# A token-group relabelling, a new vector order, and a reordered first and last pair in a convolution and SwiGLU kernel

## Chip, cores and metric

The kernel runs on one core of one Trainium2 chip. The metric is device microseconds of one execution. TensorE (PE) does the matmuls; VectorE (DVE), ScalarE (ACT) and GpSimd (POOL) work on 128-partition tiles; DMAs are issued from the queues of SyncE (SP), ScalarE and GpSimd. Everything is float32.

## The reference

```
w   = softmax(weight, axis=-1)                       # weight: 8 heads x 7 taps
y   = causal conv of x with w, one set of taps per head of 24 channels   # x: 8 x 4096 x 192
rms = sqrt(mean(y*y, axis=-1) + 1e-6)                # y as 32768 tokens x 192
xn  = y / rms * rms_g
g, val = xn @ w_gate, xn @ w_val                     # 192 x 1536 each
out = (g * sigmoid(g) * val) @ w_out                 # 1536 x 192
```

## The kernel before

**Pairs.** The 32768 tokens are cut into 32 pairs of 1024 tokens, each of two groups of 512. Pair 0 is computed plainly: `plain` (its matmuls are L1110) makes gate and value products, ScalarE the silu, VectorE the product of both, and `outer` (L1151) the output product; its results leave PSUM by a ScalarE copy (L1159) and a VectorE sum (L1163). Pairs 1 to 31 go by a bilinear scheme that needs fewer multiplications: sums of input columns ("X sums", XSUM, `x_sum` L718), of input weights (`w_sums` L375, negations L371) and of output weights (`out_sums` L914, negations L910) are formed, TensorE multiplies them, and sums of the products give the wanted values.

**One scheme pair on TensorE.** `Pair.products` yields 180 steps: 120 product steps (`Unit.product`, L823: four units u of hidden channels, 15 products i each, on two halves of the partitions), then 60 output steps (L1002), one for each word of OUTS. A word "n.u" multiplies form n of unit u by output weights; the forms (LEFT) are either the six gated blocks a to f of a unit or sums of them (SUMS: ab, cb, be, df, de, p4, p9, abe, abd, bce, bcf). The gated blocks are six (three columns of hidden channels for each of two token groups); PLACE says which block is which, and which token group is stored as g.

**The order of everything else.** ORDER is a string of words between the PE steps. "p3" is three PE steps. Another word has an engine letter and a name: V, P and W are VectorE, A ScalarE, G GpSimd, Q an accumulating DMA issued from GpSimd's queue (L1025; it reads one tile from SBUF and adds it to another), D a DMA of SyncE. A word that ends in "-" is for the pair before the current one (its tail: JOIN L1049, TURN transposes L1015, stores, and the convolution, norm, and X sums that feed later pairs). `AS`, `AF` copy PSUM (L772), `VC`, `VD`, `VN`, `VR` are VectorE sums (VR: L857), `AG` is silu (L869), `GM`/`VM` the gate product (L877), `Gab.0` and the like form sums (L1027). `Ak...` copies a summand to PSUM with ScalarE (`stage`, L726) so that the `P` sum on VectorE reads one operand there. `Asq`, `Vred`, `Gpow`, `Vbc`, `Gmul` and `Dplace` are the norm two pairs ahead (L498, L509 to L511, L515 to L521, L528, L536, L676), `cv` the convolution taps (ScalarE starts one, L474, VectorE adds six, L482), `GX1` and so on the X sums of the next pair, `load`, `fetA`, `fetB` DMAs. Each engine runs its own instructions in the order in which they were written, and waits where an input is not there. So the place of a word relative to others of its engine, and to the PE steps that use it, sets what waits.

**First pair and head.** START is a string of one-letter steps, one piece each: p, s, v are product, silu and value product of the plain pair, w four operations of `w_sums`, i, o, O weight conversions, c, n, t convolution, norm and placing of pair 1. LATER puts further steps at times of a list kept in `put`/`emit`, and so do the lines behind it for `part_tap`, `x_sum` and `out_sums` (12 of its 18 operations at `base + 2600 + 60 * i`; the rest inside pair 1's loop, one each ten PE steps after step 30). The list's numbers only order the work; they are not times on the chip.

**Last pair.** The loop runs one pass more than there are pairs, and the pass behind the last pair issues only the words that end in "-". In the last pair both stores, `st0` and `st1`, use ScalarE's queue for every second transfer.

Of the kernel before, what the change touches and what calls it, by code (L numbers as in the profile page):

```python
# [19 lines left out]
def kernel(  # L20
# [76 lines left out]
    ORDER = (
        "VD6- VD0- GX5- GX10- p1 VT2- p1 GX9- VD2- VD3- VT4- p2 VT5- Asq- AS40.0.0 p2 AS40.1.0",
        "VT3- p1 AF0.0.0 VT0- GX8- p1 VT1- VC.0.0 GX7- AF0.1.0 p3 VC.1.0 AS41.0.0 AS41.1.0 p1",
        "AS00.0.0 p2 AS00.1.0 p2 GX4- p1 Vred- VD5.1.0 AS42.0.0 VD5.0.0 p1 AS42.1.0 VR1.0.0",  # L100
        "VR0.0.0 Gpow- VR1.1.0 AS51.0.0 p1 AS51.1.0 p1 VR0.1.0 p1 Dload- Vbc- AF2.0.0 p1 AG0.0.0",
        "AF3.0.0 AG1.0.0 VN.1.0 p1 VR2.0.0 GM0.1.0 p1 AF3.1.0 p2 AG2.0.0 AS44.1.0 VR2.1.0 p2",
        "Dst1- p1 VS44.0.0 p1 VR3.0.0 p2 AS40.0.1 VR3.1.0 AS40.1.1 p1 GM1.1.0 VR5.0.0 Gmul-",
        "AG4.0.0 GM2.1.0 VR5.1.0 VM4.1.0 AG3.0.0 p1 AF0.0.1 p1 GM3.1.0 p2 Gcb.0 p1 VS41.0.1 p1",
        "AF0.1.1 VC.0.1 p1 AS41.1.1 VC.1.1 AS00.1.1 AG5.0.0 p1 VS00.0.1 p2 AS42.1.1 VS42.0.1",
        "VD5.0.1 AS51.0.1 p1 VD5.1.1 GM5.1.0 p1 AS51.1.1 p1 Gab.0 p2 VR1.0.1 p1 VR1.1.1 p1",
        "AF2.0.1 p1 AF2.1.1 VR0.0.1 p1 VR0.1.1 AG0.0.1 Qbe.0 VF3.0.1 Gdf.0 p3 VR2.0.1 GM0.1.1 p1",
        "AF3.1.1 VR2.1.1 p1 AG1.0.1 AS44.0.1 AS44.1.1 p1 VR5.0.1 AG5.0.1 GM1.1.1 p1 VR3.0.1 p1",
        "AS40.0.2 p2 VR5.1.1 VS40.1.2 p1 VR3.1.1 p2 Gde.0 p3 AG4.0.1 GM5.1.1 AF0.0.2 VM4.1.1",
        "VF0.1.2 AG3.0.1 VC.0.2 AS41.0.2 p2 VC.1.2 AS41.1.2 AG2.0.1 p1 AS00.0.2 p1 VS42.0.2 Gab.1",  # L110
        "p1 GM3.1.1 AS00.1.2 AS42.1.2 p2 VD5.0.2 p4 VD5.1.2 VR1.0.2 AS51.0.2 GM2.1.1 p1 VR1.1.2",
        "AS51.1.2 p2 VR0.0.2 AF2.0.2 p1 AF2.1.2 p1 VR0.1.2 p1 AG1.0.2 AG0.0.2 AF3.1.2 Gcb.1 p1",
        "VF3.0.2 VR2.0.2 VR2.1.2 AS44.0.2 p1 Gdf.1 Qde.1 GM1.1.2 VR5.0.2 AS44.1.2 VR5.1.2 p3",
        "AG2.0.2 p4 VR3.0.2 VS40.1.3 GM0.1.2 AS40.0.3 AG5.0.2 AG4.0.2 VR3.1.2 p1 AF0.0.3 p1",
        "AS41.0.3 p2 Gab.2 VM4.1.2 VF0.1.3 VC.0.3 p1 GM2.1.2 p1 VC.1.3 AS41.1.3 p4 GM5.1.2",
        "VS42.0.3 p1 AS00.0.3 AS00.1.3 VD5.0.3 VD5.1.3 p1 AG3.0.2 Gcb.2 AS42.1.3 p1 VR1.0.3",
        "VR1.1.3 p1 Dst0- AS51.0.3 AS51.1.3 p1 Gdf.2 Gp4.1 AF2.0.3 p1 AF2.1.3 AG1.0.3 VR0.0.3 p1",
        "VR0.1.3 p2 AF3.0.3 AF3.1.3 VS44.0.3 VR5.0.3 p1 GM3.1.2 p1 AG0.0.3 p1 AS44.1.3 VR2.0.3 p2",
# [1254 lines left out]
```

## Time and profile before

| | before |
|---|---|
| median of 3 runs | 2606.48 us (2603.78 to 2611.65) |
| the profiled execution's own time | 2604.78 us |
| its span in the profile | 2602.9 us |
| mean granted TensorE clock | 0.999 |
| busy: PE, DVE, POOL, ACT | 99%, 93%, 92%, 72% of the span |
| PE starts of scheme pairs 1, 2, 3, 4, 31 | 125.0, 212.3, 291.5, 371.4, 2516.5 us |
| last matmul starts, span ends | 2594.64 us, 2602.9 us |

In lines of the profile the columns are: start (in a timeline) or nothing, busy us, engine, line of the kernel, operation, output <- input by name, shape, and count; the square bracket is the engine's idle time before it and what ended that. In the list of waits: what waited, on which line, for which producer, us in total, number of waits, the longest.

### The profile page before, as it was taken

To read this page: it belongs to the slowest core of one execution; us is meant where nothing else is said; L and a number is where in the kernel's file an instruction comes from. 1 tells how busy PE (TensorE), PEld (TensorE's weight loads), DVE (VectorE), ACT (ScalarE), POOL (GpSimd) and SP (SyncE) were. 2 spreads that over 40 slices of the span, in tenths; PEclk is the share of its full clock that TensorE was granted. 3 is DMA by queue.
4 is the path that set the end of the run, shared out by engine and by line. 5 is a ranking of instruction groups with operands and counts; after the bars stand their busy time and mean duration, and the time that the engine had idled before them with its cause. 6 is when DMAs were issued, how large, how long until landed. Compare 5 with 4: busy or idle time off the path is not lost.

```text
span 2602.9 us, 61832 instructions
## 1 busy us (share of the span) xinstructions
PE 2564.1 (99%) x23128; PEld 1467.9 (56%) x23128; DVE 2424.1 (93%) x4056; ACT 1877.9 (72%) x3505; POOL 2398.9 (92%) x2104
## 2 busy tenths in 40 slices
PE   9999999999999999999999999999999999999998
PEld 6855555655555556555555555655556555645554
DVE  8889999999999999999999999999999999999976
ACT  6577777777777777677777777777778777787765
POOL 4899999999999999899999999999999999999987
PEclk9999999999999999999999999999999999999999
DMA  6243554444544445444455444455444455443432
GB/s 144 57 81 67 104 97 87 85 77 90 104 91 82 79 75 104 92 86 87 72 98 104 90 81 76 81 104 96 88 85 77 89 104 91 82 83 71 90 78 50
DMA packets 528490, 226.28 MB, mean 87 GB/s; under 512 B 456638, under 2 KB 459198, under 8 KB 528190
## 3 DMA queue, kind: packets, MB, share of 16 engines
q1 hardware_dynamic: 481004, 140.53, 27.4%
q0 software_dynamic: 44496, 81.02, 18.5%
q8 instruction: 182, 2.98, 0.5%
q10 hardware_dynamic: 2690, 0.79, 0.1%
q14 instruction: 118, 0.97, 0.1%
HBM read 83.84 MB, written 49.55 MB: 51 GB/s over the span
## 4 chain that ended last, share of the span: by engine, by line
PE 71%; POOL 15%; DMA 5%; issue 3%; DVE 2%; ACT 2%; SPq 0%; POOLq 0%; DVEq 0%; ACTq 0%
PE ps L823 51%; PE ps L1002 16%; POOL ht L877 5%; POOL nt L1027 3%; POOL early L1027 3%; PE ps L1110 2%; DMA early<-ht 2%; DMA more<-early 2%; PE ps L1151 1%; POOL tls L1027 1%; DMA xb<-xd 1%; POOL more L1025 1%; POOL more L1027 1%; ACT ps L772 0%; ACT ps L726 0%
## 5 line engine op out<-in xcount | busy, mean ns | idle before, releaser
L823 PE MATMUL ps<-xc,wf 64*128 64x512 f32 x4960 | 1398.1, 592 | 0.9 <-ACT tile L772 0.8
L823 PEld LDWEIGHTS ps<-xc,wf 64*128 64x128 f32 x4960 | 683.2, 187 | 462.4 <-issue 269.6
L823 PE MATMUL ps<-xb,wf 64*128 64x512 f32 x2480 | 864.9, 590 | 0.0
L772 ACT ACTIVATE tile<-ps 128x512 f32<-128x512 f32 (+1 forms) x749 | 416.3, 572 | 201.9 <-PE ps L1002 100.1
L823 PEld LDWEIGHTS ps<-xb,wf 64*128 64x128 f32 x2480 | 375.9, 187 | 241.0 <-issue 179.5
L772 ACT ACTIVATE ps<-ps 128x512 f32<-128x512 f32 (+1 forms) x713 | 383.1, 546 | 176.8 <-PE ps L1002 148.2
L772 ACT ACTIVATE tls<-ps 128x512 f32<-128x512 f32 (+1 forms) x615 | 344.1, 572 | 168.7 <-PE ps L1002 83.8
L877 POOL TENSOR_TENSOR ht<-ht,tile 128x512 f32<-128x512 f32 x312 | 438.8, 1471 | 22.0 <-ACT tile L869 21.1
L1002 PE MATMUL ps<-ht,x 128*32 128x256 f32 x5952 | 413.0, 380 | 0.0
L877 POOL TENSOR_TENSOR ht<-ht,tls 128x512 f32<-128x512 f32 x246 | 349.0, 1468 | 22.8 <-ACT tls L869 22.0
L1027 POOL TENSOR_TENSOR early<-early,ht 128x512 f32<-128x512 f32 x248 | 351.3, 1527 | 0.0
L482 DVE SCALAR_TENSOR_TENSOR ps<-xh,tp,ps 128x512 f32<-128x512 f32 x450 | 337.3, 751 | 15.1 <-ACT ps L474 8.8
L1027 POOL TENSOR_TENSOR early<-ht 128x512 f32<-128x512 f32 x248 | 342.7, 1382 | 4.8
L1002 PE MATMUL ps<-early,x 128*32 128x256 f32 x4216 | 278.9, 379 | 0.1
L1002 PEld LDWEIGHTS ps<-ht,x 128*32 128x32 f32 x5952 | 192.1, 110 | 130.1 <-DVE ht L877 4.9
L857 DVE TENSOR_TENSOR tile<-ps,tile 128x512 f32<-128x512 f32 x344 | 233.0, 684 | 11.0 <-ACT tile L772 6.3
L869 ACT ACTIVATE tile<-tile 128x512 f32<-128x512 f32 x344 | 213.9, 625 | 7.6 <-DVE tile L857 4.4
L857 DVE TENSOR_TENSOR ht<-ps,tile 128x512 f32<-128x512 f32 x310 | 209.9, 680 | 0.7 <-ACT tile L772 0.5
L857 DVE TENSOR_TENSOR tls<-ps,tls 128x512 f32<-128x512 f32 x276 | 187.3, 684 | 8.6 <-ACT tls L772 5.0
L726 ACT COPY ps<-ht 128x512 f32<-128x512 f32 x248 | 145.3, 589 | 60.2 <-DVE y L482 44.9
L1002 PEld LDWEIGHTS ps<-early,x 128*32 128x32 f32 x4216 | 136.6, 110 | 91.9 <-ACT ps L772 5.0
L869 ACT ACTIVATE tls<-tls 128x512 f32<-128x512 f32 x276 | 171.8, 625 | 6.0 <-DVE tls L857 3.6
(174 smaller groups left out, 3897.3 us busy)
## 6 DMA issues: line engine op xcount, KB each, us to landing
xb<-xd SPq DMA_DIRECT2D x120, 384.0 KB
ht<-ht POOLq DMA_DIRECT2D x93, 256.0 KB, 3.9
early<-ht POOLq DMA_DIRECT2D x93, 256.0 KB, 4.6
xd<-yn SPq DMA_DIRECT2D x244, 96.0 KB
out_dram<-o_sb SPq DMA_DIRECT2D x244, 96.0 KB
xh<-in_x_dram SPq DMA_DIRECT2D x192, 105.0 KB
more<-ht POOLq DMA_DIRECT2D x62, 256.0 KB, 3.3
more<-early POOLq DMA_DIRECT2D x31, 256.0 KB, 3.9
```

Of the source, the lines that this page charges most:

```text
L482: nc.vector.scalar_tensor_tensor(out=dst, in0=xk, scalar=w, in1=at, op0=ALU.mult, op1=ALU.add)
L726: nc.scalar.copy(out=bank(*at)[:], in_=src)
L772: nc.scalar.activation(out=dst, in_=src, func=AF.Copy, scale=float(s))
L823: nc.tensor.matmul(out=self.new(v, h, True) if first else self.old(v, h), lhsT=wf[self.u][HALF[h], WAT[i], :], rhs=x_op(XOP[i])[HALF[h]], ...
L857: nc.vector.tensor_tensor(out=dst, in0=self.old(v, h), in1=t[:], op=plus(s))
L869: nc.scalar.activation(out=t[:], in_=src[:], func=AF.Silu)
L877: engine[eng].tensor_tensor(out=self.hv(v), in0=src, in1=t[:], op=ALU.mult)
L1002: nc.tensor.matmul(out=to[q * Q : (q + 1) * Q, :], lhsT=left[:, u, a], rhs=cols[:, i * HALFT : (i + 1) * HALFT], start=fresh, stop=True, s ...
L1025: nc.gpsimd.dma_start(out=dst, in_=b, accum_op=ALU.add)
L1027: engine[eng].tensor_tensor(out=dst, in0=a, in1=b, op=ALU.add)
L1110: nc.tensor.matmul(out=bank(h, bks[h])[:], lhsT=wf[u][HALF[h], AT[h][k] * NF + f, :], rhs=xb[HALF[h], g, k, :], start=(k == 0), stop=(k == ...
L1151: nc.tensor.matmul(out=bank(h, bks[h])[:, w : w + D], lhsT=hts[f // NF][HALF[h], g, f % NF, j * P : (j + 1) * P], rhs=wo_sb[HALF[h], f, :] ...
```

## The change

The assignment of the six blocks turns: a, b, c come from the second token group and d, e, f from the first. BANKS, SIDE, OUTS and ORDER are new accordingly (the last two in every row; here the rows that are spoken of). The negations of `w_sums` and `out_sums` move from GpSimd to ScalarE. START holds four more `w`, LATER four fewer. `out_sums` is issued as 7, 8 and 3 operations at other places of the list, all of them before the loop over the scheme pairs, and the loop over pair 1 issues none. For the last pair `last` takes joins, transposes and stores out of their places and puts each as soon as its inputs, by NEEDS, have been issued; the loop has no extra pass; and of the last pair only `st1` uses ScalarE's queue. Per pair, ORDER has VectorE 117 words for 124, ScalarE 117 for 109, GpSimd 53 sums and 8 DMAs for 51 and 10.

```diff
--- before.py
+++ after.py
@@ -87,45 +87,44 @@
 
 
     SPAN = 1509
-    PLACE = {'a': 1, 'b': 0, 'c': 2, 'd': 4, 'e': 3, 'f': 5}
-    BANKS = {'K': 1, 'R': 1, 'N': 0, 'C01': 1, 'C34': 0}
+    PLACE = {'a': 3, 'b': 4, 'c': 5, 'd': 0, 'e': 1, 'f': 2}
+    BANKS = {'K': 0, 'R': 1, 'N': 1, 'C01': 0, 'C34': 1}
     OUTS = (
-        "11.1 11.0 6.0 6.2 4.1 6.1 6.3 11.2 4.2 1.0 1.2 11.3 4.0 4.3 14.3 9.0 8.0 8.1 8.2 9.1 9.3",
-        "9.2 14.2 14.1 5.0 8.3 10.0 5.3 10.3 5.1 5.2 3.1 13.2 13.1 3.3 7.0 7.3 13.0 10.1 7.1 10.2",
-        "7.2 13.3 1.3 14.0 12.0 3.0 2.1 12.1 12.3 12.2 1.1 3.2 0.3 2.2 2.0 0.1 0.2 2.3 0.0",
+        "11.0 11.1 6.0 6.3 6.2 6.1 11.2 4.2 4.0 4.1 1.1 11.3 1.2 1.0 9.0 14.0 4.3 9.2 9.1 8.1 9.3",
+        "8.2 8.3 8.0 5.1 3.1 3.3 5.0 5.2 5.3 10.2 14.3 10.1 13.2 7.1 13.0 13.3 7.2 13.1 14.1 3.2",
+        "7.3 7.0 10.3 1.3 2.0 3.0 10.0 12.2 12.3 12.1 14.2 12.0 2.2 2.3 2.1 0.2 0.1 0.3 0.0",
     )
     ORDER = (
...
-        "VR0.0.0 Gpow- VR1.1.0 AS51.0.0 p1 AS51.1.0 p1 VR0.1.0 p1 Dload- Vbc- AF2.0.0 p1 AG0.0.0",
...
-        "Qp9.2 p1 Pp9.0 Vcv1_1 Pp9.1 Gcb.3 p1 Gp9.3 p1 Vcv2_1 AF1 p1 Vcv3_1 Vcv4_1 p2 Akabe.1",
...
-        "Pbcf.1 Qabd.0 p2 AS7 Pabd.1 p2 Vcv2_0 Gbcf.2 p1 AS13 p2 Akbcf.3 Pbcf.3 VD13 AkX6 Akabd.2",
...
+        "AS00.1.0 p1 AS00.0.0 p2 VD5.1.0 AS42.0.0 AS42.1.0 VD5.0.0 p2 AS51.1.0 p1 Gpow- p2",
+        "AS51.0.0 VR1.0.0 GX7- p1 VR0.0.0 AF2.0.0 p2 VR0.1.0 VR1.1.0 p1 AG1.0.0 VN.1.0 AF3.0.0",
...
+        "VR3.1.3 p2 Akde.3 Akdf.3 Akp9.2 Pp4.2 p1 VR5.1.3 AG5.0.3 VM4.1.3 Pdf.3 p1 Dload- AS6",
+        "Pde.3 p2 DfetA p3 Akab.3 Akp9.1 Akp4.3 p2 AF3 Pp9.2 GM3.1.3 Pab.3 Pp4.3 Acv0_2 Acv0_0",
+        "GM5.1.3 p1 DfetB p1 Dst1- Pp9.1 p2 Gcb.3 p1 Gp9.3 Vcv1_2 Qbe.3 AF1 p1 Vcv2_2 p1 Vcv1_0",
...
+        "AkX0 Qabd.2 Vcv6_0 VD1 p4 Gbcf.2 p1 Akabd.0 Pabd.3 Akbcf.1 PX0 p1 Pabd.0 Qabd.1 p1",
...
     )
 
     cst = ctx.enter_context(tc.tile_pool(name="cst", bufs=1))
@@ -368,9 +367,7 @@
         t = wf[u]
         for i, (d, op, a, b) in enumerate(WSUM):
             if op == "neg":
-                nc.gpsimd.tensor_scalar(
-                    out=t[:, d, :], in0=t[:, a, :], scalar1=-1.0, scalar2=None, op0=ALU.mult
-                )
+                nc.scalar.mul(t[:, d, :], t[:, a, :], -1.0)
             else:
                 nc.gpsimd.tensor_tensor(
                     out=t[:, d, :], in0=t[:, a, :], in1=t[:, b, :],
@@ -907,9 +904,7 @@
         for d, op, a, b in VSUM:
             dst = right(d)
             if op == "neg":
-                nc.gpsimd.tensor_scalar(
-                    out=dst, in0=right(a), scalar1=-1.0, scalar2=None, op0=ALU.mult
-                )
+                nc.scalar.mul(dst, right(a), -1.0)
             else:
                 nc.gpsimd.tensor_tensor(
                     out=dst, in0=right(a), in1=right(b),
@@ -917,7 +912,7 @@
                 )
             yield
 
-    SIDE = (1, 0, 0)
+    SIDE = (0, 1, 1)
     regs = held + [more[:, i] for i in range(2)]
     REG = {"AB": 0, "CB": 1, "X": 2, "S": 3}
 
@@ -1064,7 +1059,7 @@
                 for i in range(NQ):
                     rows = slice(r + i // 2 * HALFT, r + (i // 2 + 1) * HALFT)
                     cols = slice(i % 2 * D // 2, (i % 2 + 1) * D // 2)
-                    q = nc.scalar if i % 2 and p == PAIRS - 1 else nc.sync
+                    q = nc.scalar if i % 2 and p == PAIRS - 1 and act == "st1" else nc.sync
                     q.dma_start(
                         out=out[rows, cols].rearrange("(b p) d -> p b d", p=Q),
                         in_=o[i * Q : (i + 1) * Q],
@@ -1235,12 +1230,12 @@
 
     START = (
         "XxxxxxxXdDdDdDddTTTTTTTTaakKkkaaakKkKbkKkbKbbbffpffpfsipsvivpsipisvipsvcpvowsivOcwps"
-        "iwpvsicwpsiwvpisvivcpsocvpwispvswcipvwsipsiwOvpsiwvipsvvpswopsvcpsvOnovoOpsonvOpsnoOvnopso"
+        "iwpvsicwpsiwvpisvivcpsocvpwispvswcipvwsipsiwOvpsiwvipsvvpswopsvcpsvOnovowOpsonwvOpsno"
+        "wOvnopswo"
     )
     LATER = (
         (30, "s"), (35, "v"), (45, "v"), (47, "O"), (50, "O"), (53, "O"), (55, "n"), (60, "t"),
-        (463, "w"), (564, "w"), (664, "w"), (764, "w"), (864, "w"), (964, "w"), (1064, "w"),
-        (1164, "w"), (1264, "w"),
+        (463, "w"), (564, "w"), (664, "w"), (764, "w"), (864, "w"),
     )
     heat(taps[:].rearrange("p h k -> p (h k)"), 1)
     heat(unity, 14)
@@ -1316,24 +1311,58 @@
     for i, at in zip((0, 1, 7, 2, 3, 5, 6, 10, 8, 9, 4), xat):
         put(at, functools.partial(x_sum, i))
     wsum = out_sums()
-    later(wsum, *[base + 2600 + 60 * i for i in range(12)])
+    later(wsum, *[base + 964 + 80 * i for i in range(7)])
+    later(wsum, *[base + 2520 + 40 * i for i in range(8)])
+    later(wsum, *[base + 2910 + 10 * i for i in range(3)])
     emit(float("inf"))
 
     for h in range(2):
         free[h].sort(key=lambda i: (h, i) in whole)
     order = [w for row in ORDER for w in row.split()]
+    NEEDS = {
+        "D6": "F4 S6", "D0": "S8 F0", "D2": "S2 F4", "D3": "S2 F3", "D1": "S5 F1",
+        "D13": "S13 S6", "D7": "S7 S6", "T0": "3 D0", "T1": "10 D1", "T2": "1 D13 D7",
+        "T3": "14 D3", "T4": "0 F4", "T5": "F4 D2 D6", "st0": "T0 T1 T2", "st1": "T3 T4 T5",
+        "S2": "2",
+    }
+
+    def last(order, outs):
+
+        got, row, n = set(), [], 0
+        ends = {w.split(".")[0]: i for i, w in enumerate(outs)}
+        late = [w.strip("-") for w in order if w.strip("-")[1:] in NEEDS]
+        for w in order:
+            if w[-1] == "-":
+                row.append(w)
+                continue
+            if w[1:] in NEEDS:
+                continue
+            for w in ["p1"] * int(w[1:]) if w[0] == "p" else [w]:
+                row.append(w)
+                if w[0] != "p":
+                    got.add(w[1:])
+                else:
+                    n += 1
+                    got.update(k for k, i in ends.items() if i + 121 == n)
+                more = True
+                while more:
+                    more = [w for w in late if got.issuperset(NEEDS[w[1:]].split())]
+                    for w in more[:1]:
+                        late.remove(w)
+                        row.append(w)
+                        got.add(w[1:])
+        assert not late
+        return row
+
     past = None
-    for p in range(1, PAIRS + 1):
-        now = Pair(p) if p < PAIRS else None
-        done_to = 0
+    for p in range(1, PAIRS):
+        now = Pair(p)
+        if p == PAIRS - 1:
+            order = last(order, " ".join(OUTS).split())
         for w in order:
             if w[0] == "p":
                 for _ in range(int(w[1:])):
-                    if now:
-                        next(now.line)
-                    done_to += 1
-                    if p == 1 and done_to > 30 and done_to % 10 == 0:
-                        next(wsum, None)
+                    next(now.line)
                 continue
             eng, name = w[0], w[1:]
             of = now
```

## The prediction

> **What bounds the kernel now.** I read the page first (engine shares, then the list of groups), then what TensorE waited for, then the timelines of one steady pair, of the end and of the head.
>
> ```profile
> span 2602.9 us, 61832 instructions
> ...
> PE 2564.1 (99%) x23128; PEld 1467.9 (56%) x23128; DVE 2424.1 (93%) x4056; ACT 1877.9 (72%) x3505; POOL 2398.9 (92%) x2104
> ```
>
> TensorE is the bound, with VectorE and GpSimd close under it. From the PE timeline a pair takes 120 product steps at 0.429 us and 60 output steps at 0.432, 51.5 + 25.9 = 77.4 us. Pairs start at 125.0, 212.3, 291.5, 371.4 ... 2516.5: the first scheme pair takes 87.3 us, later ones 79.18 (median). Start to start, less these pitches, TensorE loses on average 2.05 us per steady pair; 0.73 of it stands where products and output steps change over (0.51 after step 119, 0.11 after 179, 0.11 at 0), in every pair, so about 1.3 us a pair, some 39 us over 30 pairs, is the most that a better order can win. What is lost has names:
>
> ```profile
> engine line waited for: us in total, times, longest us
> PE ps L1002 <- POOL nt L1027: 9.8, 32, 1.3
> PE ps L1002 <- DMA more<-early: 7.1, 6, 3.0
> PE ps L1002 <- DMA early<-ht: 5.3, 8, 0.9
> ```
>
> The first is output word 9.3 (GpSimd) at step 140, about 0.43 us of excess per pair; the second is word 9.2, formed by an accumulating DMA, at step 141, 0.25 on average; the third is Qabd.0 near step 175, 0.24. GpSimd's place in a steady pair (this one starts at 1326.9):
>
> ```profile
> 1333.44 0.20 POOL L515 TENSOR_SCALAR r<-r 128x8 f32<-128x8 f32 x1 [1.43 <-DVE r L511]
> 1333.72 1.66 POOL L518 TENSOR_TENSOR r<-r,nhalf 128x8 f32<-128x8 f32 x1
> 1335.45 0.35 POOL L521 COPY s<-r 128x32 f32<-128x32 f32 x2
> 1337.07 1.28 POOL L877 TENSOR_TENSOR ht<-ht,tls 128x512 f32<-128x512 f32 x1 [1.27 <-ACT tls L869]
> ```
>
> The bracket is idle time and who ended it. After pow GpSimd stands 1.27 us until ScalarE's silu, then starts the first gate product 10.15 us after the pair's start. From there to Gp9.3 it has 46.5 us of work ahead and few gaps, so Gp9.3 starts 60.05 us after the pair's start and TensorE's step 140 catches it.
>
> The first scheme pair and the head:
>
> ```profile
> 190.00:194.00 4.00, 0.91 (x12) 0.36 (x16) 2.46 (x4) 0.00 (x0) 3.34 (x4) 0.95 0.68 123
> 194.00:197.00 3.00, 3.00 (x32) 1.38 (x28) 0.75 (x1) 1.99 (x4) 0.00 (x0) 0.50 0.73 174
> ```
>
> Columns: us, busy PE, PEld, DVE, ACT, POOL, granted clock, DMA share, GB/s. In pair 1 GpSimd's first gate product starts 13.2 us after the pair's start instead of 10.15, and six of the output-weight sums (0.7 us each) lie in its loop; word 9.2 is 3.18 us late (190 to 194), and then the clock stands at 0.50 for 3.4 us (1.7 lost).
>
> ```profile
> 103.96 6.52 POOL L375 TENSOR_TENSOR wf<-wf 128x128 f32<-128x128 f32 x13
> ...
> 111.54 10.49 POOL L375 TENSOR_TENSOR wf<-wf 128x128 f32<-128x128 f32 x17
> ```
> ```profile
> 107.64 0.69 ACT L474 ACTIVATE ps<-xh,tp 128x512 f32<-128x512 f32 x1 [7.39 <-POOL wf L375]
> ```
> ```profile
> 116.83 0.71 DVE L718 TENSOR_TENSOR xc<-xb 128x512 f32<-128x512 f32 x1
> ...
> 122.50 0.77 DVE L718 TENSOR_TENSOR xc<-xb,xc 128x512 f32<-128x512 f32 x1
> ```
>
> The chain ahead of pair 1 is: scaled tokens yn on GpSimd (end 104.04), ScalarE's next tap start (107.64), VectorE's taps, the mean square, then the sums X0 to X10 on VectorE; TensorE starts pair 1 at 125.0. The end:
>
> ```profile
> 2595.30 0.76 DVE L1049 TENSOR_TENSOR ps<-ps,tile 128x256 f32<-128x256 f32 x2 [1.23 <-ACT tile L772]
> 2596.10 1.77 DVE L1015 STREAM_TRANSPOSE o_sb<-ps 128x256 f32<-128x256 f32 x5
> 2597.24 2.10 SPq L1068 DMA_DIRECT2D out_dram<-o_sb  x4
> 2597.24 2.16 ACTq L1068 DMA_DIRECT2D out_dram<-o_sb  x4
> ```
>
> Five transposes and all eight stores stand behind the last output step (2594.65 to 2595.25); the span ends 7.6 us after it.
>
> **The change, part by part.**
>
> **Last pair.** Joins, transposes and stores come as soon as their inputs are there; four stores (st0) go out earlier on SP's queue. Left behind the last step: S2, one join, one transpose (0.41) and four stores on two queues. Four transposes (1.4) go ahead, and half the stores' queueing. Stores took 4.8 us from issue to the last landing with eight; with four between half and all of it. I take −3.1 (bounds −1.4, the transposes alone, to −4).
>
> **Head.** Thirteen more of the input-weight sums are put ahead of yn on GpSimd. From 85.75 its list is then: four conversions 8.2, 13 sums at 0.505 = 6.6, factor 2.4, yn 2.8, so yn ends at 105.7 at the earliest (+1.7). Earlier sums, with VectorE reading SBUF beside them, took 17.7 us for 17; at 1.04 each yn ends 8.6 later. I take +3.5. The negations move to ScalarE, and there the last two stand ahead of the tap start of 107.64: they wait for GpSimd's other sums, about 7.6 us behind yn, so that tap starts at about 115.8 (+8.1). VectorE's chain behind it (9.2 to the first X sum, 6.5 to X6) then gives pair 1's first step at 131.4: +6.4 (bounds +4.5 to +10). Queued behind ScalarE's wait are the evacuations of the plain pair, so TensorE waits about 4 us at 117.5 also; that lies inside the 6.4.
>
> **Pair 1.** GpSimd now reaches its first gate product at about 138.1, 6.7 us after the new start, ahead of the 10.15 that a steady pair needs, and no weight sums are in its loop (all 18 are issued before). So pair 1 should take a steady 79.2: −8.1, half clock included (bounds −4, if only the wait and its half clock go, to −8.1). Head and pair 1 together: −1.7.
>
> The row says that a 3.2 us wait was followed by 3.4 us at 0.50. By the Trainium skill's "TensorE: Matmul & The Clock Gate", What's actually happening, an idle window of about 3.4 us halves the clock until a busy window has passed. By that rule the new wait of 4 us at 117.5 would cost 1.7 more; it would still be hidden, since the outer products would end at about 131.0, before X6. The trace holds it to be no sure thing: a wait of 3.16 us at 1066 to 1072 left the clock at 1.00.
>
> **Steady pairs.** The swap of token groups itself is relabelling: 180 steps of the same shapes. Counts by pitch of each engine's rows, per pair: VectorE 124 to 117 operations, 72.95 to 69.0 us; ScalarE 109 to 117, 54.6 to 58.4; GpSimd 61 both, but 53 computing and 8 DMAs for 51 and 10, 71.7 to 73.0. Moved one by one: 9.2 is now a ScalarE copy and a VectorE sum used at step 137, so its DMA wait goes: −0.25 a pair, −7.5 in all. Gp9.3 has the same 46.5 us ahead of it and the same step 140: its 0.43 stays. The remaining DMAs were issued as little as 13 steps (5.6 us) ahead of use and now at least 16 (6.9), against 3.3 to 7.2 from issue to landing; the wait near 175 can go too (0.24), but I leave it, because GpSimd's queue, which issues them, is fuller. SP's loads and stores move to other places in the order, far from use: nothing. VectorE gains 4 us of slack and is not waited for in the table above: nothing. ScalarE's 8 more operations take 75% of a pair: nothing, unless a copy is late for the VectorE sum behind it. GpSimd's extra X sum, GX7 (1.23 us), stands right behind pow, in the 1.27 us gap: nothing if it fits. What an unseen order can cost is bounded by the rows: −1.3 a pair (all of the excess) to +1.7 (GX7 late by itself, 1.23, plus another DMA wait the size of 9.2's mean twice over), −39 to +51 over 30.
>
> **Sum.** 2604.8 (profiled execution: span 2602.9 and 1.9 around it) −3.1 −1.7 −7.5 = 2592.5. The median of the three runs, 2606.5, is 1.7 above the profiled one, so the forecast is 2594. Its own range is 2580 to 2602, by the bounds of end and head and half the steady term's.
>
> **Rivals.**
>
> *GpSimd becomes the bound (slower).* GX7 fills a gap of 1.27 to within 0.04 us and is itself used at step 24 (24 × 0.429 + 0.1 = 10.4 us after the pair's start), just when it is done. If pow or VectorE's r comes later (its row shows 1.43 us of waiting already), GX7 and the gate product slide, Gp9.3 with them, and nothing in the 46.5 us behind gives it back. It decides from a first gate product later than 10.15 after the pair's start; each 0.1 us costs 3 us. Half a microsecond gives 2609; the whole 1.23 gives 2594 + 37 = 2631. For: POOL at 92%, its work per pair up by 1.3. Against: GpSimd idles 7.9 us per steady pair, and other idle places (0.35 at each DMA issue) shrink with two DMAs fewer. The "SBUF — State Buffer" page of the Trainium skill (SBUF: two separate sides) says that a VectorE operation with two SBUF inputs locks GpSimd out for the whole instruction. The head's weight sums fit it, 0.505 alone and 1.04 beside VectorE; fewer such VectorE sums speaks for the change there, by an amount no row gives.
>
> *All avoidable waits go.* −1.3 ×30 instead of −7.5 gives 2604.8 − 3.1 − 1.7 − 39 + 1.7 = 2563; with Gp9.3's half of it left, 2575. For: DMA waits and margins. Against: equal work ahead of Gp9.3.
>
> *Nothing changes in the steady pairs, or the head eats the gain.* New small waits for old: 2601.5. Head at its worst bound (+10, −4) with the 7.5 won: 2594 + 7.7 = 2601.7. That the groups swap and the order only relabels is this case too.
>
> **Chances.** Forecast 0.42, all waits gone 0.12, nothing or head 0.20, GpSimd 0.26. What can be told from no change is 0.3%, 7.8 us: below 2598.7 is faster. Faster: most of the forecast (0.38) and the second rival, 0.50. Same, up to 2614.3: the third rival and a little of the others, 0.22. Slower: 0.28, GpSimd and unknown waits of an order that is new in every step. The range 2568 to 2632 leaves out about 0.06 below and 0.12 above.
>
> **What would show it.** After the change: no wait "more<-early" in pair 1 or at 9.2; "nt" still at 9.3; clock full in pair 1, which lasts about 79 and starts near 131; four stores behind the last step. I am wrong if GpSimd's first gate product starts later than 10.15 us into a pair, if pairs take other than about 78.9, or if TensorE waits for VectorE or ScalarE rows that are not in the table now.

## Result

The changed kernel takes 2612.4 us (median of 19 runs, 2611.2 to 2619.1) against 2603.6 before (19 runs, 2600.9 to 2611.7): ratio 1.0033, 95% interval 1.0026 to 1.0039. It is slower by 0.33%, 8.9 us, where 12.5 us less were forecast. The profiled executions show where. The cuts are the start of TensorE's first matmul of each scheme pair and the start of its last output step:

| us | before | after | difference | forecast |
|---|---|---|---|---|
| start of pair 1 | 125.00 | 129.38 | +4.4 | +6.4 |
| pair 1 | 87.29 | 84.19 | −3.1 | −8.1 |
| 29 pairs, 2 to 30 (mean) | 2304.3 (79.46) | 2308.7 (79.61) | +4.4 | −7.3 |
| last pair, first to last step | 78.09 | 83.01 | +4.9 | −0.2 |
| end behind the last step | 8.22 | 5.58 | −2.6 | −3.1 |
| span | 2602.85 | 2610.83 | +8.0 | −12.3 |

The page of after, the shares:

```profile
span 2610.8 us, 61741 instructions
...
PE 2575.4 (99%) x23128; PEld 1529.6 (59%) x23128; DVE 2317.2 (89%) x3838; ACT 1960.2 (75%) x3761; POOL 2415.4 (93%) x2096
```

VectorE fell from 93% to 89% and ScalarE and GpSimd rose, as counted. What TensorE waited for, after (the views of before are in the prediction):

```profile
PE ps L820 <- POOL xc L715: 10.6, 30, 0.4
PE ps L820 <- DVE o_sb L1158: 2.7, 1, 2.7
...
PE ps L997 <- ACT ps L769: 1.9, 1, 1.9
PE ps L997 <- ACT tile L769: 1.8, 3, 1.2
PE ps L997 <- DVE ps L1044: 1.1, 1, 1.1
```

The three lines shown before (Gp9.3 and the two DMAs) are gone. A new first line stands 30 times: L715 is an X sum on GpSimd. The others are waits of one place each, in the head and in the last pair.

**Steady pair.** The same stretch of GpSimd as before, in the pair that starts at 1328.07, and TensorE's third step (step 2, counted from 0; four matmul records are two steps):

```profile
1335.22 0.20 POOL L512 TENSOR_SCALAR r<-r 128x8 f32<-128x8 f32 x1 [2.04 <-DVE r L508]
1335.50 1.66 POOL L515 TENSOR_TENSOR r<-r,nhalf 128x8 f32<-128x8 f32 x1
1337.23 0.35 POOL L518 COPY s<-r 128x32 f32<-128x32 f32 x2
1337.54 1.27 POOL L715 TENSOR_TENSOR xc<-xb,xc 128x512 f32<-128x512 f32 x1
1338.93 2.51 POOL L874 TENSOR_TENSOR ht<-ht,tile 128x512 f32<-128x512 f32 x2
```
```profile
1328.07 1.13 PE L820 MATMUL ps<-xc,wf 64*128 64x512 f32 x4
1329.56 1.13 PE L820 MATMUL ps<-xc,wf 64*128 64x512 f32 x4 [0.36 <-POOL xc L715]
```

GX7 does fit the gap behind pow, and step 24 never waits for it. But step 2 waits for X10. Medians over 27 pairs, from the timelines: before, the first gate product starts 10.15 us into the pair, X10 starts 68.40 us later, takes 1.27, and ends 0.64 us into the next pair; step 2 is due at 0.96, so 0.3 us are to spare. After, the first gate product starts at 10.87 (0.62 of it is the pair's own wait at step 2) and X10 starts 68.82 later: it ends 1.43 into the next pair, and step 2 is 0.5 us late. Excess is the time between the starts of two steps beyond the pitch of 0.429 or 0.432 us. By mean excess per pair: gone are 0.43 at step 140, 0.25 at 141 and 0.24 at 175; new are 0.62 at steps 2 and 3, 0.34 at step 130 and 0.14 at 134. The mean excess is 2.06 before and 2.21 after. Round the ring from step 2 to the first gate product, to X10, and back to step 2, the medians add up to 9.19 + 68.40 + 1.27 = 78.86 us before, below that kernel's period of 79.18, and to 9.38 + 68.82 + 1.27 = 79.47 after, which is its period of 79.53 but for 0.06.

**Last pair.** TensorE, ScalarE and VectorE near its end, after:

```profile
2590.25 0.43 DVE L1044 TENSOR_TENSOR ps<-ps,tile 128x256 f32<-128x256 f32 x1
2590.73 0.64 PE L997 MATMUL ps<-ht,x 128*32 128x256 f32 x8 [1.11 <-DVE ps L1044]
...
2603.03 0.45 DVE L1010 STREAM_TRANSPOSE o_sb<-ps 128x256 f32<-128x256 f32 x1
2603.51 0.37 ACT L769 ACTIVATE ps<-ps 128x256 f32<-128x256 f32 x1 [0.98 <-DVE o_sb L1010]
...
2603.93 1.93 PE L997 MATMUL ps<-ht,x 128*32 128x256 f32 x32 [1.85 <-ACT ps L769]
...
2605.93 0.45 DVE L1010 STREAM_TRANSPOSE o_sb<-ps 128x256 f32<-128x256 f32 x1 [0.64 <-PE ps L997]
2606.41 0.88 ACTq L1063 DMA_DIRECT2D out_dram<-o_sb  x2
```

One transpose and half the stores are left behind the last step, as said. But TensorE stops in front of three output steps (152, 167 and 176), 1.32 + 0.75 + 2.04 us by excess: a join or a transpose now stands ahead of them in the same PSUM bank. The first two steps add into C1, and wait for the join D0 and the transpose T0 of C0, the other half of that bank. The third, the first into C4, needs ScalarE's copy F4, which waits for the transpose T3 of C3, again the other half. Four microseconds are paid for 2.6.

**Head.** ScalarE, after:

```profile
114.08 0.51 ACT L370 ACTIVATE wf<-wf 128x128 f32<-128x128 f32 x2 [11.05 <-POOL wf L372]
114.50 0.67 ACT L471 ACTIVATE ps<-xh,tp 128x512 f32<-128x512 f32 x1
117.33 0.42 ACT L907 ACTIVATE x<-x 128x256 f32<-128x256 f32 x1 [2.15 <-POOL x L909]
```

The negations wait for GpSimd and hold the tap start to 114.50, as forecast (115.8). TensorE starts pair 1 at 129.38, as soon as X6, the seventh X sum, is done (129.23). But after three steps it waits 3.3 us more for a PSUM bank, whose VectorE evacuation stands behind all eleven X sums (at 133.68). The last five of these take 1.10 to 1.21 us each, beside GpSimd's output-weight sums, where they took 0.68 to 0.77 before. Then the clock falls (us, busy PE, PEld, DVE, ACT, POOL, granted clock, DMA share, GB/s):

```profile
132.00:134.00 2.00, 0.00 (x0) 0.00 (x0) 2.00 (x3) 0.22 (x1) 2.00 (x3) 1.00 0.00 0
134.00:136.00 2.00, 1.72 (x6) 1.06 (x8) 0.98 (x4) 0.38 (x1) 1.92 (x4) 0.77 0.00 0
136.00:138.00 2.00, 2.00 (x7) 1.02 (x5) 1.13 (x2) 0.73 (x2) 2.00 (x1) 0.50 0.00 0
```

### The profile page after: what moved, and what is told of

It reads as the page before. It is cut to its first block, busy times and chain, and to the rows that moved or that the text cites. A ratio compares the mean times of both kernels' runs of the same rounds, so it can differ in the third digit from the quotient of the medians.

```text
span 2610.8 us, 61741 instructions
## 1 busy us (share of the span) xinstructions
PE 2575.4 (99%) x23128; PEld 1529.6 (59%) x23128; DVE 2317.2 (89%) x3838; ACT 1960.2 (75%) x3761; POOL 2415.4 (93%) x2096
## 4 chain that ended last, share of the span: by engine, by line
PE 63%; POOL 24%; issue 4%; ACT 4%; DMA 2%; DVE 2%; ACTq 0%; POOLq 0%; DVEq 0%
PE ps L820 59%; POOL early L1022 12%; POOL xc L715 6%; PE ps L1105 2%; DMA xb<-xd 2%; ACT ps L723 2%; POOL ht L874 2%; POOL nt L1022 1%; POOL early L1020 1%; POOL ht L1020 1%; PE ps L997 1%; ACT tile L866 1%; ACT ps L769 1%; PE ps L1146 1%; DVE tile L854 0%
## 5 line engine op out<-in xcount | busy, mean ns | idle before, releaser
L820 PE MATMUL ps<-xc,wf 64*128 64x512 f32 x4960 | 1364.5, 595 | 14.1 <-POOL xc L715 10.6
L820 PE MATMUL ps<-xb,wf 64*128 64x512 f32 x2480 | 819.2, 590 | 0.0
L769 ACT ACTIVATE ps<-ps 128x512 f32<-128x512 f32 (+1 forms) x775 | 415.6, 551 | 153.4 <-PE ps L997 122.4
L769 ACT ACTIVATE tile<-ps 128x512 f32<-128x512 f32 (+1 forms) x807 | 442.1, 573 | 109.3 <-PE ps L820 41.1
L874 POOL TENSOR_TENSOR ht<-ht,tile 128x512 f32<-128x512 f32 x361 | 493.7, 1406 | 13.6 <-ACT tile L866 8.1
L769 ACT ACTIVATE tls<-ps 128x512 f32<-128x512 f32 (+1 forms) x712 | 391.0, 569 | 106.0 <-PE ps L997 38.7
L1022 POOL TENSOR_TENSOR early<-early,ht 128x512 f32<-128x512 f32 x310 | 441.7, 1676 | 0.4 <-PE ps L997 0.4
L997 PE MATMUL ps<-ht,x 128*32 128x256 f32 x5952 | 390.6, 380 | 8.4 <-ACT ps L769 1.9
L874 POOL TENSOR_TENSOR ht<-ht,tls 128x512 f32<-128x512 f32 x228 | 325.3, 1442 | 16.0 <-ACT tls L866 9.7
L866 ACT ACTIVATE tile<-tile 128x512 f32<-128x512 f32 x371 | 232.5, 630 | 1.8
L854 DVE TENSOR_TENSOR ht<-ps,tls 128x512 f32<-128x512 f32 x277 | 188.0, 680 | 2.9
```

Of the source, the lines that this page charges most:

```text
L769: nc.scalar.activation(out=dst, in_=src, func=AF.Copy, scale=float(s))
L820: nc.tensor.matmul(out=self.new(v, h, True) if first else self.old(v, h), lhsT=wf[self.u][HALF[h], WAT[i], :], rhs=x_op(XOP[i])[HALF[h]], ...
L854: nc.vector.tensor_tensor(out=dst, in0=self.old(v, h), in1=t[:], op=plus(s))
L866: nc.scalar.activation(out=t[:], in_=src[:], func=AF.Silu)
L874: engine[eng].tensor_tensor(out=self.hv(v), in0=src, in1=t[:], op=ALU.mult)
L997: nc.tensor.matmul(out=to[q * Q : (q + 1) * Q, :], lhsT=left[:, u, a], rhs=cols[:, i * HALFT : (i + 1) * HALFT], start=fresh, stop=True, s ...
```

## Experiments

In the expectations "the wait at step 2" means two things: step 2 (X10) in the steady pairs, and the long wait behind step 2 in pair 1. A profile is of one execution, and so is the time of a run without a ratio. Kernels with the same head and the same steady order (after, old_last, last_late_joins) start pair 1 at 129.0 to 130.5 and end it at 213.1 to 213.6, so smaller differences there are not read. The kernels by the same cuts, us:

| kernel | start | pair 1 | mean of 29 | last pair | end | span |
|---|---|---|---|---|---|---|
| before | 125.00 | 87.29 | 79.46 | 78.09 | 8.22 | 2602.9 |
| after | 129.38 | 84.19 | 79.61 | 83.01 | 5.58 | 2610.8 |
| x3_dve | 129.46 | 86.22 | 85.28 | 84.03 | 5.57 | 2778.4 |
| red_early | 129.05 | 84.19 | 80.72 | 82.76 | 5.58 | 2642.4 |
| old_last | 129.05 | 84.19 | 79.60 | 78.85 | 8.14 | 2608.5 |
| last_late_joins | 130.54 | 82.55 | 79.66 | 78.91 | 6.04 | 2608.3 |
| negs_pool | 130.14 | 83.58 | 79.64 | 82.91 | 5.57 | 2611.7 |
| negs_both | 127.99 | 85.45 | 79.63 | 83.05 | 5.59 | 2611.3 |
| sums_late | 129.88 | 84.28 | 79.62 | 82.50 | 5.58 | 2611.3 |
| start_before | 130.33 | 83.58 | 79.62 | 83.02 | 5.58 | 2611.4 |
| head_before | 124.63 | 82.27 | 79.63 | 83.00 | 5.57 | 2604.7 |
| order_only | 125.38 | 82.71 | 79.66 | 78.81 | 8.15 | 2605.1 |
| before_cb_twice | 124.79 | 85.81 | 82.02 | 78.11 | 8.19 | 2675.5 |
| x3_early | 128.95 | 86.00 | 80.72 | 82.33 | 5.59 | 2643.7 |
| x3_unstaged | 129.77 | 86.22 | 83.05 | 82.35 | 5.59 | 2712.3 |
| gate_dve | 128.92 | 84.19 | 79.23 | 82.61 | 5.60 | 2599.0 |
| gate_combo | 125.21 | 82.56 | 79.24 | 78.38 | 6.03 | 2590.2 |
| s6_combo | 125.78 | 82.45 | 79.25 | 78.48 | 6.05 | 2591.0 |

### The last pair

```diff
 old_last:
-        if p == PAIRS - 1:
-            order = last(order, " ".join(OUTS).split())
+    (the loop with its extra pass, and both stores on two queues, as before)
```

> After, with the last pair done as before (no early joins and stores, a last pass for them, both stores on two queues). Theory A (the joins put ahead of output steps that add into the same PSUM bank make TensorE wait 1.3 + 0.6 + 2.0 us): last pair 79.4 to 79.6 instead of 83.0, end 8.2 instead of 5.6 after the last step: total 1.0 us less. Rival B (the last pair is long because its GpSimd work is late): last pair stays at 83, total 2.6 us more.

Measured: last pair 78.85, end 8.14; together 1.6 us less than after. The three waits are gone. last_late_joins keeps the early stores and only delays joins:

```diff
-"D0": "S8 F0", "D1": "S5 F1", "D3": "S2 F3", "S2": "2"
+"D0": "S8 F0 3 10", "D1": "S5 F1 3 10", "D3": "S2 F3 0", "S2": "2 F4"
```

> After, with four entries of the last pair's list of needs made stricter: the joins of the banks that two parts share wait for the last output step that adds into either part, and the copy S2 for the copy F4. Theory A (a join or transpose ahead of an output step into the same PSUM bank makes TensorE wait): the last pair falls from 83.0 to 79.4 to 79.6 us, and one join and one transpose (0.9) more stand behind the last step, 6.4 to 6.6 instead of 5.6; total 2.5 to 2.8 us less, about 2609.7. Rival B (the wait is for ScalarE's queue): last pair above 81.

Measured: last pair 78.91 and no wait above 0.6 us in it, end 6.04 (expected 6.4 to 6.6). The pair and its end take 84.95 us, against 88.59 after and 86.31 before. So early stores are worth 2.0 us over the old end of the same order (86.99 in old_last), once no join stands ahead of an output step into its bank. These four delays are all that was changed, so the early joins and the copy S2 are where the 4.1 us of waits came from.

### The head

```diff
 head_before: START, LATER, the places of out_sums and both negations from before
              (six output-weight sums in pair 1's loop again)
```

> After, with the whole head as before: the order of the first pair, the weight sums' places (six of the output-weight sums inside pair 1's loop) and the negations on GpSimd. Theory A (the new head costs more at the start, 4.4 + 3.3 + 1.7 us, than it saves in pair 1's loop): pair 1 starts at 125.0 without a wait at step 2 above 1 us; pair 1 takes 79.5 plus what six sums of 0.7 us push: up to 84; total 4 to 8 us less than after. Rival B (the saving in pair 1 is as big as the loss): total within 1 us of after.

head_before: start and pair 1 together end at 206.9 instead of 213.6: the new head costs 6.7 us, with the new order in both. (Below, order_only, gate_combo and s6_combo have the old head too and end pair 1 at 207.8 to 208.2, so 5 to 7 us is what the profiles support.) And pair 1 with the old head takes 82.3 where before it took 87.3: the new ORDER, without the DMA wait for 9.2 and the half clock behind it, gained 5 us there. Then one part of the head at a time:

```diff
 negs_pool     w_sums:   -nc.scalar.mul(...)  +nc.gpsimd.tensor_scalar(... -1.0 ...)
 negs_both     the same in w_sums and out_sums
 start_before  START, LATER of before
 sums_late     out_sums at the places of before (six in pair 1's loop)
```

> After, with the negations of the input-weight sums back on GpSimd. Theory A (two negations on ScalarE's queue, waiting for GpSimd's last weight sums, hold back the tap start behind them): the tap start stands right behind the scaled tokens and their DMAs, at about 110.5 instead of 114.5, and TensorE's pair 1 starts some 4 us earlier, near 125.5, with a smaller wait at step 2; total 3 to 6 us less. Rival B (yn, 2.8 us later than before, sets the start): pair 1's start moves by under 1 us.

> After, with both kinds of negation, of input weights and of output weights, back on GpSimd. In negs_pool the output-weight negation was the next to hold ScalarE (6.6 us, to 119.4). Theory A (the negations on ScalarE hold the tap start, the mean square and the copies of the plain pair): tap start at about 112, mean square at about 117.5 instead of 120, X sums from 121, pair 1's start 127 to 128 with the wait at step 2 still there; total 2 to 4 us less than after. Rival B (GpSimd's and VectorE's order in the head sets it): under 1 us.

> After, with START and LATER alone as before (13 of the input-weight sums behind the scaled tokens again); output-weight sums and negations as after. Theory A: the tokens are scaled by 104, the tap start stands at 108 or behind a negation at up to 111, X sums start 117 to 120, pair 1 starts 125 to 127; total 3 to 6 us less. Rival B (the places of the output-weight sums and the negations hold the head): X sums start above 122, total within 1.5 us of after.

> After, with the output-weight sums alone placed as before (12 behind the X sums in the list, six in pair 1's loop); START, LATER and negations as after. Theory A (the new head's cost has two parts: the tokens and the tap start come 7 us later by START and the negations, and the output-weight sums on GpSimd slow VectorE's X sums beside them from 0.7 to 1.2 us each): X sums start near 123 still, but take 0.7 to 0.9 us each, the wait at step 2 falls from 3.3 to below 1.5, and no half clock follows it; total 2 to 5 us less. Rival B (the X sums are slow for another reason): wait at step 2 still above 3.

| us | yn done | tap start | mean square | first X sum | pair 1 ends |
|---|---|---|---|---|---|
| after | 106.9 | 114.5 | 120.0 | 123.7 | 213.6 |
| negs_pool | 107.9 | 112.1 | 120.1 | 123.8 | 213.7 |
| negs_both | 108.2 | 112.0 | 117.5 | 121.2 | 213.4 |
| start_before | 103.9 | 109.6 | 120.3 | 124.0 | 213.9 |
| sums_late | 107.4 | 115.0 | 120.5 | 124.2 | 214.2 |
| head_before | 103.7 | 107.4 | 112.8 | 116.6 | 206.9 |

All four expectations of a gain failed: no part alone gives back more than 0.2 us. Where ScalarE is concerned, holds stand one behind another on its queue. Take the first away and the next ends at nearly the same time. In start_before the tap start comes 5 us earlier, but the output-weight negation then waits 7.8 us for GpSimd and the second pair of input-weight negations stands behind it, so the mean square, whose input is there at 115.0, starts at 120.3:

```profile
118.12 0.42 ACT L907 ACTIVATE x<-x 128x256 f32<-128x256 f32 x1 [7.83 <-POOL x L909]
119.48 0.51 ACT L370 ACTIVATE wf<-wf 128x128 f32<-128x128 f32 x2 [0.94 <-POOL wf L372]
...
120.25 1.49 ACT L495 ACTIVATE yn<-y 128x1536 f32<-128x1536 f32 x1
```

In negs_both the negations hold nothing, but the scaled tokens are late by START; pair 1 starts 1.4 us earlier than in after, and a longer half-clock stretch (6.8 us for 3.4; pair 1 is 1.3 us longer) takes that back. In sums_late the wait behind step 2 only fell to 2.8 us. Four of the output-weight sums still ran from 128.0 to 132.6, since the X sums come late, and the X sums beside them still took 1.1 to 1.2; the last X sum, behind them, took 0.68. No half clock followed, but the six sums in pair 1's loop cost it 1.4 us at step 130 and 0.65 at step 80. Undone together, the parts give 6.7. Which two of them would be enough was not run.

### The steady pairs

```diff
 order_only: before, with PLACE, BANKS, SIDE, OUTS and ORDER of after
```

> Before, with only the group assignment, OUTS, ORDER, BANKS and SIDE of after; head, negations and last pair as before. Theory A (three parts add up: the head costs 6.7 us, the last pair 1.6, the new order gains 5 in pair 1 and loses 4 to 5 over 29 pairs): start 124.6, pair 1 82.3, 29 pairs 2308 to 2309, last pair 78.9, end 8.1: span 2602 to 2603, no difference from before. Rival B (the new order is the loss, whatever the head): more than 2607.

order_only takes 2605.8 against 2603.2 (ratio 1.0009, interval 1.0000 to 1.0018). So the order by itself is no gain and hardly a loss: by the cuts, 4.6 us are gained in pair 1, 5.8 lost in the 29 pairs, 0.7 in the last pair and 0.4 at the start.

```diff
 red_early: -"VC.0.0 AS41.0.0 p2 VC.1.0 p1 Vred- p1"   +"Vred- VC.0.0 AS41.0.0 p2 VC.1.0 p2"
```

> After, with VectorE's mean-square reduction moved ahead of its two VC sums, so that pow can start up to 2 us earlier. Theory A: GpSimd's 2.0 us of idle time before pow shrinks by at least 0.6, the wait at step 2 goes, period 78.9 to 79.0. Rival B: VectorE's VC sums come 2.4 us later and TensorE waits for their banks instead; period 79.5 or more.

pow started 1.7 us earlier in the pair, and it did not help: the wait at step 2 stayed at 0.53, TensorE got a new wait of about 1.2 us at steps 10 to 12 for VectorE, and the first gate product started at 11.90 instead of 10.87, because silu (L866), behind VectorE's late sums, now ends its wait:

```profile
PE ps L820 <- DVE tile L846: 15.4, 19, 0.9
```
```profile
1351.04 1.27 POOL L715 TENSOR_TENSOR xc<-xb,xc 128x512 f32<-128x512 f32 x1
1355.17 1.27 POOL L874 TENSOR_TENSOR ht<-ht,tile 128x512 f32<-128x512 f32 x1 [2.86 <-ACT tile L866]
```

The period rose by 1.1 us, as much as that start. In after, the gate product starts 0.12 us behind GX7 and 0.24 behind the end of silu; where silu alone releases it, in before, it starts 0.15 behind. So an earlier pow could win about 0.1 us at most: the loop that sets the period runs from the first gate product to X10, and pow is hardly in it. The theory's first link was wrong there; the rest is tested next.

Three attempts took X3 (1.23 us) off GpSimd:

```diff
 x3_dve:      -"PX1 p1 PX2 ... Vcv6_1 GX3 VD2"    +"PX1 AkX3 p1 PX2 ... Vcv6_1 PX3 VD2"
 x3_early:    -"PX0 p1 Pabd.0 ... Pbcf.1"         +"PX0 AkX3 p1 Pabd.0 ... Pbcf.1 PX3"
 x3_unstaged: -"PX0 p1 Pabd.0 Qabd.1"             +"PX0 p1 Pabd.0 VX3 Qabd.1"
```

> After, with one of GpSimd's X sums (X3, the last GpSimd word of a pair) given to VectorE, its summand staged in PSUM by ScalarE. Theory A (GpSimd's loop sets the period: pow, 59 GpSimd operations, X10, TensorE's step 2, VectorE's mean square, pow again): 1.23 us less per loop, so the wait of 0.5 us at step 2 goes, the period falls from 79.53 to 78.9 to 79.0 us, the whole by 15 to 18 us, to about 2595. Rival B (X10 is only placed late, and the next late word takes its place): the wait turns up at output word 9.3 or another, period above 79.3, total above 2606.

> After, with X3 given to VectorE (staged by ScalarE) early enough, about 17 output steps before the pair's end, so that GpSimd's chain X6, X5, X10 does not wait for it. In x3_dve it stood at the pair's end and the chain waited for it; that run did not test the theory. Theory A (GpSimd's work from its first gate product to X10 sets the wait at step 2): 1.23 us less work ahead of X10, the wait of 0.52 + 0.10 us goes, period 78.9 us, total 2594 to 2596. Rival B (another late word takes its place): period 79.3 to 79.6, total above 2605.

> After, with X3 on VectorE reading both summands from SBUF, about 17 steps before the pair's end, with no copy by ScalarE and no PSUM bank. In x3_early the wait at step 2 was gone, and the bank and ScalarE's queue made another of 1.8 us at step 165. Theory A: without the bank neither wait, period 78.9 to 79.1 us, total 2594 to 2599. Rival B (a VectorE sum with two SBUF operands holds GpSimd up for as long as it lasts, and its own wait moves the chain): GpSimd loses 0.7 us, period 79.2 to 79.5.

All three are slower. x3_dve (ratio 1.0636, 1.0607 to 1.0665) put X3 at the end of the pair, where X6, X5 and X10 then waited for it: it doesn't test the theory. In x3_early the wait at step 2 is gone, as the theory says, but step 165 waits 1.8 us for ScalarE, whose queue stands 1.2 us for VectorE's X sum; by that releaser, for the PSUM bank that the sum gives back. In x3_unstaged step 170 waits 1.9 us and the wait at step 2 grows to 1.7: VectorE's sum with two SBUF operands takes 3.96 us, where its neighbours with one operand in PSUM take 0.68:

```profile
1119.76 0.68 DVE L1022 TENSOR_TENSOR early<-early,ps 128x512 f32<-128x512 f32 x1
1120.36 3.96 DVE L715 TENSOR_TENSOR xc<-xb 128x512 f32<-128x512 f32 x1
```
```profile
1120.35 3.40 POOL L1022 TENSOR_TENSOR early<-early,ht 128x512 f32<-128x512 f32 x2
```

The extra moves made waits of their own; the price of GpSimd's 1.23 us stayed open after them. gate_dve takes as much off it without a copy, a bank more or a second SBUF operand:

```diff
-"VR3.1.3 p2 Akde.3 ...    Pp9.2 GM3.1.3 Pab.3
+"WR3.1.3 VM3.1.3 p2 Akde.3 ...    Pp9.2 Pab.3
```

> After, with one gate product of GpSimd (block a of unit 3) given to VectorE; its value stays in its PSUM bank for it, so that VectorE reads one operand there and no copy and no bank is added. The three moves of X3 took the wait at step 2 away or shifted it, but each brought a wait of its own (its place, a bank, two SBUF operands), so none has priced the theory. Theory A: 1.23 us less GpSimd work between the first gate product and X10; waits at step 2 (0.62) and before Gp9.3 go, period 78.8 to 79.0, total 2592 to 2598. Rival B (the new order has late words on every engine, one behind another): period 79.3 or more, total above 2605.

Measured: the excess at step 2 falls from 0.52 to 0.03, the period from 79.53 to 79.14 (median), the single run from about 2612 to 2600.8. No "POOL xc" line is left among TensorE's waits; step 2 of a steady pair stands in one row with its neighbours, where after had the wait of 0.36:

```profile
1322.68 2.12 PE L820 MATMUL ps<-xc,wf 64*128 64x512 f32 x8
```

So GpSimd's work ahead of X10 is the cause, but its price is 0.39 us a pair and not 0.6: 0.18 stays at steps 3 and 5, and step 130 waits as before. Of the 1.23 us taken off, only 0.48 shortens the way from the first gate product to X10 (68.36 for 68.84, medians); the rest comes back as waiting of GpSimd, 0.54 ahead of a gate product 57 us into the pair and 0.23 near 62. The total lies between the two theories' numbers.

```diff
 before_cb_twice: -"GM3.1.0 p2 Gcb.0 p1"   +"GM3.1.0 p2 Gcb.0 Gcb.0 p1"
```

> Before, with one GpSimd sum of each pair (cb of unit 0) issued twice: 1.23 us more GpSimd work per pair, nothing else changed. Theory A (GpSimd's work from the first gate product on sets the period already before the change): the wait at output word 9.3 grows from 0.43 by 0.9 to 1.2 us, period 80.2 to 80.5, total 25 to 36 us more. Rival B (before, GpSimd has slack for a sum; its 7.9 us of idle time take it up): under 9 us more.

The same from the other side, in the kernel before: 1.23 us more of GpSimd cost 2.6 us a pair in the mean (82.02 for 79.46). GpSimd had no slack in either order, but theory A has the place and the size wrong. The wait at word 9.3 (step 140) stayed at 0.44; the excess came at steps 77 and 78 (0.4), 131 and 133 (0.7) and 141 (1.1):

```profile
PE ps L1002 <- DMA more<-early: 36.0, 27, 2.8
PE ps L1002 <- POOL nt L1027: 11.8, 39, 1.4
PE ps L1002 <- POOL tls L1027: 8.6, 30, 0.3
```

GpSimd's queue also issues the DMA of word 9.2, which then comes later (step 141), and the forms in tls are late too.

### A version of the parts

```diff
 combo:      head_before + last_late_joins + x3_unstaged
 gate_combo: head_before + last_late_joins + gate_dve
 s6_combo:   gate_combo, -"AG5.0.3 VM4.1.3 Pdf.3 p1 Dload- AS6"   +"VM4.1.3 Pdf.3 p1 Dload- AS6 AG5.0.3"
```

> The new order with X3 unstaged on VectorE, before's head, and the last pair of last_late_joins. Theory A: start 124.6, pair 1 81.7 to 82.3, 29 pairs at 78.9 to 79.1 (2288 to 2294), last pair 78.3 to 78.9, end 6.0: span 2580 to 2587, against 2602.9 before: 16 to 23 us less, 0.6 to 0.9% faster than before. Rival B: period 79.5 as after, span 2600.

combo was built on x3_unstaged and shares its fault (2705.3 us, ratio 1.0387, 1.0373 to 1.0401): 83.08 us a pair, and pair 1 takes 84.6 for the 82 expected, with 1.9 at step 170 there too. The last pair is as expected (78.2), the end a little longer (6.6 for 6.0). With gate_dve in its place:

> The new order with the same gate product on VectorE, before's head, and the last pair of last_late_joins. Theory A: start 125, pair 1 81.5 to 82.7, 29 pairs 2286 to 2292, last pair 78.3, end 6.0: span 2577 to 2584, 0.7 to 1.0% faster than before. Rival B: period 79.5 as after, span 2603, no difference.

gate_combo takes 2591.8 against 2602.4 (ratio 0.9959, 0.9946 to 0.9973): faster than both kernels, 0.4% and not 0.7. Its parts are what they were one by one (start 125.2, pair 1 82.6, 79.24 a pair, 78.4 + 6.0 at the end).

> gate_combo, with one silu (block f of unit 3) moved behind the copy S6 on ScalarE. Theory A (the 0.34 us at step 130 is ScalarE's queue: the silu of 0.6 us stands ahead of S6, and step 130 waits for S6): the wait at step 130 goes, period 78.8 instead of 79.14, total 9 to 10 us less than gate_combo, about 2582. Rival B (S6 waits for the copies ahead, which wait for GpSimd): period stays at 79.1.

The wait at step 130 fell from 0.33 to 0.04, but steps 131, 134 and 2 took on 0.09, 0.17 and 0.08, and the period stayed (79.25): 2592.3 against 2603.4, ratio 0.9955 (0.9941 to 0.9968). ScalarE's queue was what step 130 waited for. It bought nothing, since the next words, from VectorE at 131 and from GpSimd at 134, were as late. Theory A had the cause of the wait right and the gain wrong.

## Why the prediction was wrong

The forecast of the span was −12.3 us and +8.0 came. Of the 20.3 between them, 11.7 are in the steady pairs, 5.1 in the last pair and 5.0 in pair 1; start and end are 2.0 better and 0.5 worse than forecast.

- **End and last pair.** −3.1 forecast for the end, −2.6 measured: inside its bounds. What failed is the line that the stores and joins "come as soon as their inputs are there" with nothing in it for the output steps behind them. I had checked what a join waits for, and not what waits for the join. That cost 4.1 us of waits, 4.9 on the last pair; old_last and last_late_joins show it.
- **Head, first half.** The tap start (114.5 for 115.8) and the X sums' start (123.7 for 124.9) were right, and X6 did open pair 1, 2 us earlier than forecast (129.4 for 131.4). What the sum left out is the bank behind all eleven X sums, the second gate. Start and wait together are +7.7 (4.4 + 3.3) where 6.4 was written.
- **Pair 1.** Less its wait (3.3) and its half clock (1.6 by excess at steps 6 to 9; last_late_joins had the wait and no half clock, and takes 1.6 less), pair 1 takes 79.3, close to the steady 79.2 of the forecast. The wait of 4 us that I put at 117.5, where it would be hidden, did not come (0.3 and 0.7 there); 3.3 us came behind step 2 instead, with the half clock, where nothing hides them. And head_before shows what most of the gain is owed to: pair 1 takes 82.3 with the six sums still in its loop. These 5 us are the new order's doing (no DMA wait at 9.2, no half clock), not the weight sums'. The 3 us from there to 79.3 stand at steps 76, 80, 123 and 130 of head_before, and after, with no sums in the loop, has only 0.33 at 130 of them. So they are likely the weight sums', but after's wait of 3.3 us gave GpSimd time as well, and no run parts the two.
- **Steady pairs.** The DMA wait for 9.2 went, and the one near 175 too, as the text allowed. The failed step is "Gp9.3 has the same 46.5 us ahead of it ... its 0.43 stays". The time from the first gate product to Gp9.3 was indeed equal (49.88 before, 49.79 after, medians), but the list was not followed to its end. Behind Gp9.3, up to X10, whose user is step 2 of the next pair, stand 12 sums and 3 DMA issues for 10 and 5, 19.05 us for 18.46. From the first gate product to X10 that is 0.42 us more, and the slack was 0.3. The 0.43 at step 140 did not stay: Gp9.3 starts 0.6 us later in the pair, but TensorE, by its new waits, comes to step 140 0.6 later too.
- **The GpSimd rival** had the engine and the sign right, the place wrong. GX7 fitted; the gate product did start later than 10.15 (10.87), but that lateness is the pair's own wait seen from its start. The row on the 1.27 us gap decided nothing by itself: GX7 fits it to 0.1 us.
- **ScalarE.** "8 more operations ... nothing, unless a copy is late" was close to the wait at step 130 (0.34 a pair): a copy is late there (S6), but it is TensorE that waits for it and not a VectorE sum. I named late copies and did not price them.

## What to carry over

When work is moved on an engine that is nearly full, follow its list once round to the first consumer in the next iteration: the slack there, not at the word you watch, is what an extra operation spends. Before an operation is issued earlier, ask which later instructions touch the same bank or stand behind it in the same queue, since an in-order queue turns one early wait into everyone's. If several holds stand in parallel, undoing them one by one shows nothing; undo them together first, then add them back.

## What the runs showed of the hardware

- A VectorE sum with two SBUF operands was held up to 3.96 us (0.68 otherwise) while GpSimd ran two-operand sums back to back, and in the head of after X sums of two SBUF operands take 1.1 to 1.2 us beside GpSimd's sums, which themselves take 1.05 to 1.17 instead of 0.73. By the Trainium skill's "SBUF — State Buffer" (SBUF: two separate sides), such an operation and a GpSimd operation take the shared ports in turn, each for its whole length; the rows agree, with one thing more: GpSimd's two sums that were queued when the VectorE sum came started at 1120.35 and ended at 1123.75, and the VectorE sum ended 0.6 later, so it waited for both, not for one.
- The clock did not fall by the length of one wait alone. The same wait of 3.3 us in pair 1 was followed by a half-clock stretch in after (pair 1 84.19) and by none in last_late_joins (82.55). In x3_dve two waits of 2.1 and 1.6 us by excess (steps 0 and 2), with two steps between them, were followed by clock 0.50 in nearly every pair:

```profile
1324.00:1327.00 3.00, 1.13 (x4) 0.30 (x4) 2.96 (x9) 1.36 (x3) 2.92 (x3) 0.90 0.00 0
1327.00:1330.00 3.00, 2.18 (x6) 1.15 (x8) 0.00 (x0) 0.57 (x3) 3.00 (x3) 0.50 0.54 131
1330.00:1333.00 3.00, 3.00 (x8) 1.05 (x8) 1.29 (x3) 1.00 (x2) 1.43 (x2) 0.50 0.00 0
```

  Some 2.5 us a pair go there (0.42 us more on each of steps 4 to 7 and parts of 3, 8 and 9). "TensorE: Matmul & The Clock Gate" of the Trainium skill (What's actually happening) has a window of about 3.4 us that runs free of the work; that the same wait costs in one run and not in another agrees with it. So do the clock records of the traces: the half-clock stretch in pair 1 is 3.41 us in before and after and 6.83 in negs_both, and in x3_dve stretches of 6.83 us at half clock alternate with 78.51 (23 times 3.41) at full clock, so that its pairs take 85.3 us, 25 times 3.41. But the waits of 3.2 us (before) and 3.3 us (after), shorter than such a stretch, were enough here: a window idle from end to end was not needed. How much work keeps the clock up, no run here shows.
